# Two attention blocks on one core: output weights folded into the key-value sums, A's output kept in SBUF, full last units and a new instruction order

## The chip, the cores and the metric

One Trainium2 chip, one core. The kernel is one launch. Its time is device microseconds (us). Repeated executions of one kernel on one chip were compared with executions of the kernel before on the same chip in the same rounds. An execution is called slow when it lies over 1.5% above the fastest of its kernel, the others fast. The profile is one execution of its own, and its span is some 2 us shorter than the time of that execution (before: span 358.7, time 360.54).

## The reference

Two independent blocks, A and B, each on 2048 rows of 640 numbers in bf16, with 32 heads of 20 numbers. The two outputs are put side by side.

```python
def _A_ref(x, wqkv, wo):            # softmax attention
    qkv = (x @ wqkv).reshape(B, S, 3, H, Dh)      # then q, k, v by head
    scores = jnp.einsum("bhqd,bhkd->bhqk", q, k) * (Dh ** -0.5)
    p = _softmax(scores, axis=-1)
    o = jnp.einsum("bhqk,bhkd->bhqd", p, v)
    return o.transpose(...).reshape(B, S, D) @ wo

def _B_ref(x, wqkv, wo):            # linear attention
    phi = lambda t: jnp.where(t > 0, t + 1, jnp.exp(t)) + 1e-6
    pq, pk = phi(q), phi(k)
    kv = jnp.einsum("bhsd,bhse->bhde", pk, v)
    z = jnp.einsum("bhsd->bhd", pk)
    num = jnp.einsum("bhqd,bhde->bhqe", pq, kv)
    den = jnp.einsum("bhqd,bhd->bhq", pq, z)[..., None] + 1e-6
    return (num / den).transpose(...).reshape(B, S, D) @ wo
```

## The kernel before

The kernel does not compute A's 2048 x 2048 scores. It builds features of the keys (products up to third order), sums feature times value over all rows, builds the same features for the queries ("psi": sums and products of query rows loaded from a DRAM copy, f_Qd), and multiplies these with the sums. A "unit" is six heads by 512 query rows: twelve psi tiles against twelve tiles of sums (f_Tu). B runs beside it: key-value sums, query features, numerators and denominators.

A planner places every instruction when the program is built. It simulates the engines with assumed durations and transfer times, and when several tasks could be next it goes by a table of priorities (`_C`; a smaller number comes earlier). The result is one fixed order per engine and queue. So an edit of one step can move many other instructions.

The parts that matter here, first the end of B:

```python
        def qden(tc):                 # 512 query rows
            ...                       # 5 projections, features pqT, denominators
            m1 = self.spd([lambda e: e.dma_start(dc, self.dn[pr, :].rearrange(...))], ...)    # 32x512 -> 128x128
            e2 = self.dve(1.1, rc, (m1,), prio=0.9)                                           # reciprocal
            m2 = self.spd([lambda e, bdw=bdw: e.dma_start(bdw, dc)], (e2,), ...)              # to DRAM, f_Bd
        def numout(tc, qs, m2):
            for c in range(N_DC):     # 5 groups of 128 columns
                ...                   # 2 or 3 loads a group: reciprocals of each head to its rows, f_wB<-f_Bd
                def nmm(b, c=c):      # numerators: a block-diagonal product, 4 strips and 1 or 2 neighbours
                    self.fm(ps[:, b, :], self.kvN[:, c, 32:160], pqT[:, c, :], ...)
                    ...
                def npost(_, j=j, c=c, k=k):
                    sch.op("dve", lambda e: e.scalar_tensor_tensor(
                        oT[:, c, :], ps[:, j.bank, :], self.cn[:, c:c + 1], self.Rb[:, k, :], op0=ALU.add, op1=ALU.mult), ...)
            ...                       # out rows = oT x output weights woB
```

A's normalized output went to DRAM and back, to stand as 5 x 128 rows:

```python
        sch.op("dve", lambda e: e.tensor_tensor(self.OTw[0:120, ow], self.OTr[0:120, r:r + 3], self.Rbc[rb][0:120], op=ALU.mult), ...)
        fns = [lambda e: e.dma_start(bass.AP(od.tensor, od.offset, [[self.S, 120], [120 * self.S, nu], [1, 512]]),
                                     self.OTw[0:120, ow, 0:nu, :])]
        ...
    def t_out(self, qc, deps):
        ol = self.spd([lambda e: e.dma_start(self.OTp[:, k], self.Od.ap()[:, col].rearrange("(c p) q -> p c q", p=128))], ...)
```

And A's query weights were brought into their order by GpSimd:

```python
        def perm(_):
            for c in range(N_DC):
                sch.op("pool", lambda e, c=c: e.tensor_copy(
                    self.w[:, 0, c, 0:600].rearrange("p (b a h) -> p b a h", b=5, h=6),
                    self.w0r[:, c, 0:600].rearrange("p (b h a) -> p b a h", b=5, h=6)), ...)
```

## Time and profile before

| | before |
|---|---|
| time, median of 3 | 359.45 us (358.58 to 362.37) |
| span of the profile | 358.7 us |
| TensorE busy / idle | 303.6 / 55.1 us |
| VectorE, ScalarE, GpSimd busy | 253.3, 180.1, 31.3 us |
| DMA | 58.85 MB |
| TensorE holes over 1.9 us | 8, together 30.7 us |

### The profile page before, as it was taken

The numbers are of one execution on the slowest core, as the hardware profiler recorded it, in microseconds if no ns is written. First come the engines' busy times: TensorE is split into PE (matmuls) and PEld (weight loads), VectorE is DVE, ScalarE is ACT, GpSimd is POOL, SyncE is SP. The second block draws the span as 40 slices with busy tenths as digits, with TensorE's granted clock in tenths as the row PEclk, the third lists the DMA queues.
The fourth block names the chain that finished last, engine by engine and source line by source line (L and its number), as shares of the span: only waits on it lengthen the run. The fifth ranks groups of instructions, "written<-read, shape, count | busy, mean of one in ns | idle before, by whom it ended". The sixth has DMA issues, their size and how long they took to land.

```text
span 358.7 us, 14998 instructions
## 1 busy us (share of the span) xinstructions
PE 303.6 (85%) x6834; PEld 198.4 (55%) x6834; DVE 253.3 (71%) x350; ACT 180.1 (50%) x377; POOL 31.3 (9%) x49
## 2 busy tenths in 40 slices
PE   5989579999998899879988299982999868789955
PEld 2657347777764356546744178741554324658723
DVE  2589699999988986878896349795658767441330
ACT  2775647888884235444433235442355535335413
POOL 0049880000020100000000000000000000000000
PEclk9999989999999699998999879998799989999988
DMA  7999548214247258277736947579874466566642
GB/s 264 250 212 136 90 92 248 57 49 126 59 132 201 62 133 246 65 190 201 191 119 178 203 119 256 146 166 242 227 206 140 133 185 213 164 228 199 210 141 82
DMA packets 63571, 58.85 MB, mean 164 GB/s; under 512 B 21036, under 2 KB 59980, under 8 KB 63500
## 3 DMA queue, kind: packets, MB, share of 16 engines
q1 hardware_dynamic: 58940, 49.99, 53.9%
q10 hardware_dynamic: 4560, 7.83, 7.3%
q8 instruction: 55, 0.90, 1.2%
q14 instruction: 16, 0.13, 0.1%
HBM read 39.65 MB, written 14.48 MB: 151 GB/s over the span
## 4 chain that ended last, share of the span: by engine, by line
PE 53%; DMA 15%; DVE 11%; POOL 8%; SPq 6%; issue 5%; ACT 1%; ACTq 0%; DVEq 0%
PE ps L172 52%; DMA f_big<-f_Qd 4%; SPq L1594 4%; DMA f_w<-f_Od 4%; POOL f_w L1157 3%; POOL f_st L1248 3%; DMA f_Rc<-f_xT 2%; DMA f_dc<-f_dn 2%; DMA f_pk<-in_A_x_dram 2%; DVE f_Tu L1449 2%; DMA f_wB<-f_Bd 1%; DVE f_pk L1993 1%; DVE f_big L1607 1%; DVE f_big L1357 1%; DVE f_big L1362 1%
## 5 line engine op out<-in xcount | busy, mean ns | idle before, releaser
L1607 DVE TENSOR_TENSOR f_big<-f_big 120x1536 bf16<-120x1536 bf16 (+2 forms) x68 | 67.6, 1001 | 8.4 <-DMA f_big<-f_Qd 7.0
L172 PE MATMUL ps<-f_wB,f_xB 128*32 128x320 bf16 x1280 | 52.2, 311 | 10.1 <-issue 8.0
L172 PE MATMUL ps<-f_big,f_Tu 120*32 120x512 bf16 (+2 forms) x880 | 53.4, 384 | 3.1 <-issue 1.7
L172 PEld LDWEIGHTS ps<-f_wB,f_xB 128*32 128x32 bf16 x1280 | 37.5, 100 | 21.7 <-issue 9.6
L172 PE MATMUL ps<-f_w,f_xT 128*32 128x320 bf16 x1280 | 48.4, 307 | 0.4 <-issue 0.2
L172 PEld LDWEIGHTS ps<-f_w,f_xT 128*32 128x32 bf16 x1280 | 34.3, 100 | 11.3 <-issue 0.8
L172 PEld LDWEIGHTS ps<-f_big,f_Tu 120*32 120x32 bf16 (+2 forms) x880 | 27.7, 98 | 23.2 <-issue 3.1
L1092 ACT COPY f_xT<-ps 126x512 f32<-126x512 f32 (+1 forms) x30 | 17.4, 587 | 39.2 <-PE ps L172 32.8
L172 PE MATMUL ps<-f_wo,f_w 128*32 128x320 bf16 x640 | 25.6, 320 | 6.9 <-DMA f_w<-f_Od 6.9
L1762 ACT ACTIVATE f_ex<-ps 128x320 f32<-128x320 f32 (+1 forms) x52 | 25.7, 498 | 11.3 <-PE ps L172 6.4
L1357 DVE TENSOR_TENSOR f_big<-f_big,f_Ks 128x3200 bf16<-128x3200 bf16 x16 | 30.3, 1896 | 1.3 <-ACT f_Ks L1092 1.3
L172 PE MATMUL ps<-f_xT,f_w 128*32 128x512 bf16 (+2 forms) x440 | 28.8, 408 | 2.6 <-POOL f_w L1160 2.5
L1092 ACT CAST f_st<-ps 128x320 bf16<-128x320 f32 x32 | 13.3, 426 | 34.5 <-PE ps L172 30.2
L172 PE MATMUL ps<-f_woB,f_pk 128*32 128x320 bf16 x640 | 25.1, 312 | 6.4 <-DVE f_pk L1993 5.9
L1362 DVE TENSOR_TENSOR f_big<-f_big 128x3200 bf16<-128x3200 bf16 x16 | 29.7, 1857 | 0.0
L172 PE MATMUL ps<-f_xB,f_wB 128*32 128x512 bf16 x400 | 28.8, 392 | 0.6 <-ACT f_ex L1762 0.6
L1993 DVE SCALAR_TENSOR_TENSOR f_pk<-ps,f_cn,f_wB 128x512 bf16<-128x512 f32 x20 | 14.0, 745 | 21.7 <-PE ps L172 18.4
L1758 DVE TENSOR_SCALAR f_r<-ps 128x320 f32<-128x320 f32 x32 | 14.8, 485 | 18.2 <-ACT f_ex L1762 17.0
L1092 ACT CAST f_pk<-ps 128x320 bf16<-128x320 f32 x32 | 13.5, 429 | 26.1 <-PE ps L172 25.6
L172 PEld LDWEIGHTS ps<-f_wo,f_w 128*32 128x32 bf16 x640 | 19.3, 103 | 12.9 <-DMA f_w<-f_Od 7.9
L172 PEld LDWEIGHTS ps<-f_woB,f_pk 128*32 128x32 bf16 x640 | 17.8, 101 | 13.5 <-DVE f_pk L1993 7.9
L1627 ACT ACTIVATE f_Dq<-f_big 120x512 bf16<-120x512 bf16 (+1 forms) x24 | 15.1, 628 | 13.2 <-DMA f_big<-f_Qd 11.3
(125 smaller groups left out, 386.4 us busy)
## 6 DMA issues: line engine op xcount, KB each, us to landing
f_big<-f_Qd SPq DMA_DIRECT2D x20, 480.0 KB, 8.0
f_Qd<-f_OTw SPq DMA_DIRECT2D x40, 120.0 KB, 2.5
f_big<-f_Qd SPq DMA_DIRECT2D x20, 240.0 KB, 8.8
f_w<-f_Nd ACTq DMA_DIRECT2D x4, 720.0 KB
f_Rbc<-f_Nd ACTq DMA_DIRECT2D x4, 720.0 KB
f_wB<-f_Bd SPq DMA_DIRECT2D x12, 240.0 KB
f_w<-f_Od SPq DMA_DIRECT2D x4, 640.0 KB
out_dram<-f_st SPq DMA_DIRECT2D x16, 160.0 KB, 3.3
```

Source lines behind the costliest of these rows:

```text
L172: lambda e: e.matmul(out, lhsT, rhs, start=start, stop=stop, tile_position=tp, skip_group_check=sgc),
L1092: return self.sch.op("act", lambda e: e.copy(out, in_), reads=reads, writes=writes)
L1157: sch.op("pool", lambda e, c=c: e.tensor_copy(self.w[:, 0, c, 0:600].rearrange("p (b a h) -> p b a h", b=5, h=6), self.w0r[:, c, 0:600].re ...
L1248: ops.append((lambda e, x=x, a=a, n=n, b=b: e.tensor_copy(self.P[:, x, 6 * a:6 * (a + n)].rearrange("p (a h) -> p a h", h=6), self.ident[0 ...
L1357: sch.op("dve", lambda e: e.tensor_tensor(F[:, :, 122:222].rearrange("p h (d a) -> p h d a", a=20), k0.unsqueeze(2).broadcast_to([128, 32, ...
L1362: sch.op("dve", lambda e: e.tensor_tensor(F[:, :, 22:122].rearrange("p h (d a) -> p h d a", a=20), k0.unsqueeze(2).broadcast_to([128, 32, ...
L1594: fns.append(lambda e, x=x, d=d, st=st, nj=nj: e.dma_start(self.slot[0:40 * nj, s, x, :], self.q_load(5, qc, d, nj, st, False)))
L1607: return e.tensor_tensor(x[:, o:o + n, :], x[:, a:a + 1, :].broadcast_to([p, n, 512]), x[:, b:b + n, :], op=ALU.mult)
L1627: sch.op("act", lambda e: e.activation(self.Dq[0:120 if c < 5 else 40, dq, :], src, AF.Square), reads=(k0,), writes=(("Dq", dq),))
L1758: sch.op("dve", lambda e: e.tensor_scalar(r1, ps[:, j.bank, 0:n], 0.0, 1e-6, op0=ALU.max, op1=ALU.add), reads=(("ps", j.bank),), writes=(( ...
L1762: sch.op("act", lambda e: e.activation(ex, ps[:, j.bank, 0:n], AF.Exp), reads=(("ps", j.bank),), writes=(("ex", k, h),))
L1993: sch.op("dve", lambda e: e.scalar_tensor_tensor(oT[:, c, :], ps[:, j.bank, :], self.cn[:, c:c + 1], self.Rb[:, k, :], op0=ALU.add, op1=AL ...
```

## The change

Its intent is to take work and waits off TensorE's path. It has five structural parts, new assumed transfer times for the planner, and a new table of priorities. In the experiments below that exchange the table, the transfer times stay with the structure.

- B: M = (masked key-value sums) x (output weights) is built once. The output is then (query features x reciprocal denominators) x M, and the numerators go. The key sums z travel over DRAM to get the layout of the denominators' weights.
- Query features and M are ordered by place within a head, then by head, so the reciprocals of 32 heads are 32 rows, sent four times.
- A's normalized output is written straight into the operand of A's last projection; only heads 30 and 31 (40 of 640 rows) go over DRAM.
- These two heads, formerly four small units of 4 tiles, become full units over three or four row blocks.
- The query weights are permuted by ScalarE, for A and B.

```diff
-_C = dict(q=1.24, qs=0.0, ks=-0.005, kd=0.02, bk=1.83, bks=-0.005, bq=6.44, bo=0.03, out=0.46, pv=0.002,
-          fe=1.73, psi=5.5, r=-1.04, f=0.92, nm=2.51, op=2.71, kv=1.87, npo=2.33, bqs=0.002,
-          bd=-0.79, bn=3.42)
+_C = dict(q=1.06, qs=0.02, ks=0.02, kd=0.0, bk=1.32, bks=0.002, bq=0.33, bo=0.1, out=1.83, pv=0.05, fe=1.97,
+          psi=7.02, r=-4.28, f=0.38, nm=5.76, op=5.3, kv=1.49, npo=2.2, bqs=0.05, bd=0.02, bn=4.14)
 ... (A's query weights)
-                sch.op("pool", lambda e, c=c: e.tensor_copy(
+            self.copy(x.eng, self.w[:, 0, c, 0:600].rearrange("p (b a h) -> p b a h", b=5, h=6),
+                      self.w0r[:, c, 0:600].rearrange("p (b h a) -> p b a h", b=5, h=6), ("w0r",), (("w", 0, c),))
 ... (A's output)
+                sch.op("dve", lambda e: e.tensor_tensor(self.OTw[0:120, kw, c:c + nu, :], self.OTr[0:120, r:r + nu],
+                                                        self.Rbc[rb][0:120, 0:nu], op=ALU.mult), ...
-        self.ost[G] = self.spd(fns, (m,), (("OTw", ow),), (("Od", G),), prio=0.6)
 ... (B: the key sums, M, the denominators)
+        z1 = self.spd([lambda e: small(e, bass.AP(zd.tensor, zd.offset, [[1, 128], [128, N_DC], [1, 1]]), self.zn[:, 0, :])], ...
+        z2 = self.spd([lambda e: small(e, self.zn[:, 1, :], bass.AP(
+            zd.tensor, zd.offset, [[1, 4], [D_HEAD, N_HEADS], [4, N_DC], [1, 1]]))], (z1,), ...
+                        self.fm(ps[:, b, 0:320], self.KVT[:, c, 128 * k:128 * (k + 1)], self.woB[:, c2, hc], ...
-            m2 = self.spd([lambda e, bdw=bdw: e.dma_start(bdw, dc)], (e2,), (("dc", tc % 2),), (("Bd", tc),), ...
+            m2 = self.spd([lambda e, i=i: e.dma_start(self.Rb[32 * i:32 * i + 32, k, :].rearrange("h (j q) -> h j q", j=4), dc)
+                           for i in range(4)], ...
+                sch.op("dve", lambda e: e.scalar_tensor_tensor(
+                    pqT, pqT, 1e-6, self.Rb[:, k, :].unsqueeze(1).broadcast_to([128, N_DC, 512]), op0=ALU.add,
+                    op1=ALU.mult), ...
-                self.fm(ps[:, b, :], self.kvN[:, c, 32:160], pqT[:, c, :], start=True, stop=False, ...
+                            self.fm(ps[:, b, 0:320], pqT[:, c, 128 * tl:128 * (tl + 1)], self.Mp[:, c, hc], ...
```

## The prediction

> **What bounds the kernel now.** I began with the page: busy time by engine, and the span in 40 slices.
>
> ```profile
> PE 303.6 (85%) x6834; PEld 198.4 (55%) x6834; DVE 253.3 (71%) x350; ACT 180.1 (50%) x377; POOL 31.3 (9%) x49
> ...
> PE   5989579999998899879988299982999868789955
> ...
> PEclk9999989999999699998999879998799989999988
> ```
>
> TensorE is the busiest engine. Span minus its busy time is 358.7 - 303.6 = 55.1 us of idling. The slices put that in a few places: slices 4 and 5 (40 to 60 us), one at 200, one at 245, and the last quarter. So the time is matmul work plus holes. The table of stretches, cut at those places (columns: TensorE, weight load, VectorE, ScalarE, GpSimd busy us, granted clock, DMA share, GB/s), shows what a hole costs:
>
> ```profile
> 40.00:50.00 10.00, 5.92 (x132) 4.10 (x132) 10.00 (x7) 4.05 (x11) 9.82 (x4) 0.83 0.54 98
> ...
> 200.00:206.30 6.30, 0.04 (x4) 0.04 (x7) 0.87 (x3) 0.00 (x0) 0.00 (x0) 0.84 1.01 181
> 206.30:210.00 3.70, 3.70 (x53) 2.57 (x56) 0.00 (x0) 1.20 (x3) 0.00 (x0) 0.50 0.74 203
> 243.90:250.50 6.60, 0.08 (x8) 0.03 (x8) 3.82 (x5) 1.05 (x3) 0.00 (x0) 0.86 1.03 231
> 250.50:256.00 5.50, 5.50 (x88) 3.36 (x92) 3.13 (x3) 1.39 (x4) 0.00 (x0) 0.54 0.88 228
> ```
>
> After each of the two long holes the clock is about half for 4 to 5 us, and both holes have the DMA engines full (share 1.0). Summing idle TensorE time over 10 us stretches I get: 0-40: 6.7 us; 40-60: 6.6; 60-120: 2.6; 120-200: 7.0; 200-280: 14.6; 280-end: 17.7. The chain that ended last, in order of time (start, us, what), names what fills them:
>
> ```profile
> 39.85 2.50 POOL f_w L1157
> 42.40 2.75 POOL f_w L1157
> ...
> 236.94 13.48 DMA f_w<-f_Od
> ...
> 341.58 0.62 SPq L1972
> 342.24 4.98 DMA f_wB<-f_Bd
> ```
>
> GpSimd permutes A's query weights while Q projections wait; A's output goes to DRAM and back before its last projection; B's end waits for reciprocals broadcast from DRAM by 52 small loads, issued one after the other by SyncE. The VectorE timeline adds one thing: the same instruction before and inside the GpSimd permutation (39.9 to 52.1 us).
>
> ```profile
> 39.43 1.82 DVE L1357 TENSOR_TENSOR f_big<-f_big,f_Ks 128x3200 bf16<-128x3200 bf16 x1
> ...
> 43.95 2.88 DVE L1357 TENSOR_TENSOR f_big<-f_big,f_Ks 128x3200 bf16<-128x3200 bf16 x1
> ...
> 50.90 1.34 DVE L1269 SCALAR_TENSOR_TENSOR f_woB<-f_Rbc,f_pq 128x147 bf16<-128x147 int32 x1
> ```
>
> The product stretches from 1.82 to 2.88 us, the mask operation from 0.31 (at 39.20) to 1.34.
>
> **What the Trainium skill says.** "SBUF — State Buffer", Who interferes with whom: VectorE with two SBUF inputs and GpSimd lock each other out of a shared port pair. The stretched instructions above agree. "TensorE: Matmul & The Clock Gate", HAM oscillation: TensorE gaps above about 3.4 us bring the half clock back. The trace agrees (0.50 and 0.54 after gaps of 6.7 and 6.5 us). "DMA: Bandwidth & Descriptors", Anatomy of one DMA: a fixed cost of about 2 us on the GpSimd-issued path. These transfers are issued by SyncE and ScalarE and their small ones (64 KB, the denominators) land in 4.0 to 5.8 us, so I use those. The same page, Rules for kernel authors: a strided last dimension is one descriptor per element. That bears on the new 640-number transfers; nothing in this trace shows one.
>
> **The change, part by part.**
>
> *B's fold.* Per 512 rows the numerators took 5 groups of 4 matmuls and 8 single strips, 112 in all: 5.2 + 3.2 + 2.5 = 10.9 us (rows of f_kvN with f_xB, f_pq, f_Vp). They go, with 28 column sums (0.4). Instead the kernel builds M = (masked key-value sums) x (output weights) once: 30 transposing matmuls of 128 columns at 23 ns (the 147-column ones: 7.5 us / 320) = 0.7, and 26 groups x 4 = 104 matmuls of 320 columns at 39 ns (25.1 / 640) = 4.1 us. The output projection keeps its 640 matmuls, with normalized queries for numerators. On VectorE 20 x 745 ns = 14.0 us (L1993) go; 4 in-place products of 2560 elements come. Row L1781 takes 665 ns for 512 and 811 for 640, so 1.14 ns an element: 3.0 us each, 12.0 in all. SyncE loses 52 x 0.73 = 38 us of issuing and gets 16 issues.
>
> *Last heads as full units.* Four small units with 64 matmuls (4.2 us) go. Two units come: one full, (53.4 + 9.0) / 20 = 3.1 us, and one of 176 columns, 48 x 28 ns = 1.3. 8 more selector matmuls: about 1.0. On VectorE 4 x 1.3 = 5.2 becomes 3.2 + 1.1 = 4.3, and the normalizing products shrink from 14.0 to about 12.5. The six loads of each small unit (20 of 0.74 and 4 of 1.64 us, 21 us of issuing) become two per unit.
>
> *A's output in SBUF.* The round trip over f_Od (2.6 MB out, 2.6 back) goes, save 40 rows of 640.
>
> *Query rows by place then head.* 30 instead of 40 stored rows per head: 4.8 MB becomes 3.6.
>
> *Weights permuted on ScalarE.* 12.6 us leave GpSimd. ScalarE gets 5 x 0.8 us for A and 5 x 0.65 for B (597 ns for 608 columns, row f_Ks<-f_big), and with the copies of M about 15 us, on an engine with 180 of 359 busy. Q projections can start some 10 us earlier, and the VectorE stretching goes: 1.05 + 0.32 + 0.36 + 1.05 + 1.03 = 3.8 us.
>
> *Order.* All priorities and assumed transfer times are new; B's query projections now come early.
>
> Sums. TensorE: -10.9 - 0.4 - 4.2 + 0.7 + 4.1 + 3.1 + 1.3 + 1.0 = -5.3, so 298 us. VectorE: 253 - 14.0 + 12.0 - 3.8 - 0.9 - 1.5 = 245 us. DMA: out 5.1 (f_Bd) + 5.1 (f_Od) + 1.2 + 1.4 (small units) + 0.3; in 1.6 (M) + 1.0 (reciprocals) + about 0.3: net -10 MB of 58.85.
>
> TensorE stays the busiest, so the time is 298 plus its idling. By stretch, my judgement: 0-40: 6.7 to 5.5 (fewer GpSimd constants); 40-60: 6.6 to 1.5; 60-120: 2.6 unchanged; 120-200: 7.0 to 6; 200-280: 14.6 to 6 (the f_Od wait goes; the hole at 200 has no named releaser, but stood with full DMA engines, so I count half of it); 280-end: 17.7 to 11 (the SyncE-bound broadcast goes, the last store and one serial chain stay). That is 33 us. Fewer cold stretches take some 2 us off the busy time (3.7 x 0.50 + 5.5 x 0.46 = 4.4 today). 298 - 2 + 33 = 329. I add 5 us for waits that a new order will make and that I can't see: **334 us**.
>
> **Rivals.** *Only the matmul work counts.* New waits replace the old ones and only the 5.3 us are saved: about 353 us. For it: 85% busy, and queues that run in order wait wherever a transfer lands later than planned. Against: the three waits named on the chain are structurally gone. *A new chain at B's end.* The key-value sums (ready at 241 us) now feed two 640-number transfers over DRAM, the denominators, a transfer, a reciprocal, a broadcast and a 3 us product; beside that M goes out and back. Five serial landings of 5 to 8 us are some 35 us before B's first output. If the sums come late, the end is bare: about 362 us. Against: the assumed transfer times were raised (4 to 6, 6.5 to 8), and A's work can lie beside it. *ScalarE or VectorE holds the first stage.* VectorE is over 93% busy from 60 to 100 us; if ScalarE's added copies delay the key evictions, the gain of the first stage (5 us) is lost: about 340 us.
>
> **Range and chances.** The middle is 334. All holes closed down to about 20 us gives 318; the first rival 353. The range is 320 to 350. Faster by over 2% means below 352.3: 0.87. Same: 0.10. Slower: 0.03.
>
> **What would show it.** Right: TensorE busy 295 to 300 us; no f_kvN with 512 columns; no hole over 3 us at 40-60; no GpSimd permutation; VectorE 243 to 248; DMA about 49 MB; idling 28 to 40 us. Wrong: TensorE idle still near 50 us, with the new M, z or reciprocal transfers named in the last 80 us; or a TensorE busy time above 302.

## More of the kernel before

The experiments ran in three batches, each on a chip of its own with its own executions of the kernel before, so kernels of different batches are compared by their ratios to it and not by their times.

One more view is needed to compare with later. It lists what TensorE waited for. The columns are the total in us, the number of waits, and the longest; "issue" is a wait for which the profile names nothing.

```profile
PE ps L172 <- issue: 10.0, 6, 6.7
PE ps L172 <- DMA f_w<-f_Od: 6.9, 2, 6.5
PE ps L172 <- DVE f_pk L1993: 6.7, 7, 2.3
...
PE ps L172 <- DVE f_xB L1781: 4.8, 2, 3.4
...
PE ps L172 <- POOL f_w L1160: 2.5, 1, 2.5
```

These are, in order: a hole without a name at 200 us, A's round trip over DRAM, B's normalized numerators, B's late query features, and the weights permuted by GpSimd.

## The result

The changed kernel takes 326.08 us (median of 4, 325.31 to 329.35), the kernel before 359.01 us (4, 356.97 to 362.37) in the same rounds. The ratio is 0.912 (95% interval 0.903 to 0.921). A ratio here and below is the mean time of one kernel's fast runs over that of the kernel before's fast runs of the same rounds, so not quite the ratio of the medians quoted. All four runs of the changed kernel were fast; of the kernel before one, 362.37, counts as slow by the 1.5% rule.

The page of the changed kernel, busy time and slices:

```profile
PE 290.7 (90%) x6866; PEld 202.5 (63%) x6866; DVE 250.8 (78%) x342; ACT 191.7 (59%) x400; POOL 11.6 (4%) x35
...
PE   5989869998899989999999899999669949999994
...
PEclk9999968999999995999999999999979999999999
```

The span is 323.5 us, so TensorE idles 32.8 us; busy time fell by 12.9 us and idling by 22.3. A slice is 8.1 us; what is left of holes is in the sixth (40 to 49 us), in two at 226 to 243 and in one at 259 to 267. There are four holes over 1.9 us instead of eight, 12.5 us together. TensorE's waits, same columns as before:

```profile
PE ps L172 <- issue: 7.2, 9, 3.8
PE ps L172 <- ACT f_big L1091: 3.6, 2, 3.0
PE ps L172 <- DVE f_big L1592: 3.0, 1, 3.0
```

Of the four named waits of before none is left; what remains without a name has 7.2 us instead of 10.0. The table of stretches, cut at the new holes (TensorE, weight load, VectorE, ScalarE, GpSimd busy, granted clock, DMA share, GB/s):

```profile
41.28:44.30 3.02, 0.07 (x4) 0.00 (x0) 2.63 (x7) 2.96 (x6) 2.47 (x10) 0.87 0.41 91
44.30:49.00 4.70, 4.67 (x44) 1.71 (x48) 3.11 (x3) 3.10 (x7) 3.80 (x10) 0.50 0.59 87
223.00:233.98 10.98, 8.83 (x171) 5.93 (x172) 7.46 (x9) 5.79 (x16) 0.00 (x0) 1.00 0.73 39
233.98:237.75 3.77, 0.01 (x3) 0.00 (x1) 1.41 (x2) 0.00 (x0) 0.00 (x0) 1.00 0.78 156
```

The first hole is new in kind: ScalarE is busy in it and GpSimd no longer is the cause. Ahead of the second there is a stretch in which the DMA engines are 0.73 busy and move only 39 GB/s, where the holes of before had 181 and 231 GB/s. The chain that ended last, in order of time (start, us, what):

```profile
250.25 12.77 DMA f_dc<-f_dn
...
267.11 39.30 PE ps L172 x942
306.43 0.43 ACT f_Ks L1091
...
307.00 12.52 PE ps L172 x360
```

From 267 us on the chain is TensorE's own work. Before, the last 60 us of it were eviction, matmul, reciprocal transfer and again eviction by turns.

### The profile page after: what moved, and what is told of

The parts are those of the page before. It is cut to its first block, busy times and chain, and to the rows that moved or that the text cites. A ratio compares the mean times of both kernels' runs of the same rounds, so it can differ in the third digit from the quotient of the medians.

```text
span 323.5 us, 14990 instructions
## 1 busy us (share of the span) xinstructions
PE 290.7 (90%) x6866; PEld 202.5 (63%) x6866; DVE 250.8 (78%) x342; ACT 191.7 (59%) x400; POOL 11.6 (4%) x35
## 2 busy tenths in 40 slices
DMA packets 58757, 47.60 MB, mean 147 GB/s; under 512 B 23629, under 2 KB 57609, under 8 KB 58689
## 4 chain that ended last, share of the span: by engine, by line
PE 64%; DVE 11%; DMA 10%; ACT 9%; issue 3%; ACTq 1%; SPq 0%; DVEq 0%
PE ps L172 64%; DMA f_dc<-f_dn 4%; DVE f_big L1592 2%; ACT f_w L1091 2%; DVE f_big L1355 2%; DVE f_big L1360 2%; DVE f_Tu L1447 2%; DMA f_Nd<-f_Rc 2%; DMA f_pk<-in_A_x_dram 2%; DMA f_big<-f_Qd 2%; ACT f_Ks L1091 1%; ACT f_wB L1091 1%; ACT f_pk L1091 1%; ACT f_big L1091 1%; DVE f_kn L1365 1%
## 5 line engine op out<-in xcount | busy, mean ns | idle before, releaser
L1592 DVE TENSOR_TENSOR f_big<-f_big 120x1536 bf16<-120x1536 bf16 (+3 forms) x66 | 67.0, 1015 | 1.9 <-DMA f_big<-f_Qd 0.4
L172 PE MATMUL ps<-f_big,f_Tu 120*32 120x512 bf16 (+5 forms) x968 | 59.5, 377 | 6.3 <-issue 3.1
L172 PE MATMUL ps<-f_wB,f_xB 128*32 128x320 bf16 x1280 | 48.9, 299 | 2.1 <-ACT f_Vp L1091 1.4
L172 PEld LDWEIGHTS ps<-f_big,f_Tu 120*32 120x32 bf16 (+2 forms) x968 | 32.3, 97 | 26.1 <-issue 7.1
L1091 ACT COPY f_xT<-ps 126x512 f32<-126x512 f32 (+2 forms) x27 | 15.4, 576 | 43.9 <-PE ps L172 37.7
L1091 ACT CAST f_pk<-ps 128x320 bf16<-128x320 f32 (+4 forms) x65 | 26.0, 416 | 11.7 <-PE ps L172 11.4
L1767 ACT ACTIVATE f_ex<-ps 128x320 f32<-128x320 f32 (+1 forms) x52 | 25.6, 498 | 11.6 <-PE ps L172 5.4
L1605 ACT ACTIVATE f_Dq<-f_big 120x512 bf16<-120x512 bf16 (+1 forms) x22 | 13.6, 618 | 17.6 <-DMA f_big<-f_Qd 13.1
L172 PEld LDWEIGHTS ps<-f_wo,f_w 128*32 128x32 bf16 x640 | 18.5, 98 | 7.2 <-ACT f_xT L1091 2.1
L172 PEld LDWEIGHTS ps<-f_xT,f_w 128*32 128x32 bf16 (+2 forms) x440 | 12.2, 106 | 16.7 <-issue 5.7
L1091 ACT CAST f_qk<-ps 120x512 bf16<-120x512 f32 (+1 forms) x21 | 12.3, 585 | 14.8 <-PE ps L172 14.7
L172 PEld LDWEIGHTS ps<-f_xB,f_wB 128*32 128x32 bf16 x400 | 13.6, 96 | 11.7 <-issue 4.2
L1763 DVE TENSOR_SCALAR f_r<-ps 128x320 f32<-128x320 f32 x32 | 14.9, 486 | 7.2 <-ACT f_ex L1767 5.0
L1091 ACT COPY f_Ks<-f_big 128x608 bf16<-128x608 bf16 (+1 forms) x32 | 19.1, 597 | 1.0
```

The costliest lines, as they stand in the source:

```text
L172: lambda e: e.matmul(out, lhsT, rhs, start=start, stop=stop, tile_position=tp, skip_group_check=sgc),
L1091: return self.sch.op("act", lambda e: e.copy(out, in_), reads=reads, writes=writes)
L1592: sch.op("dve", lambda e: e.tensor_tensor(sl[:, o:o + n, :], sl[:, a:a + 1, :].broadcast_to([120, n, N]), sl[:, b:b + n, :], op=ALU.mult), ...
L1605: sch.op("act", lambda e: e.activation(self.Dq[0:120, dq, 0:N], sl[:, 0, :], AF.Square), reads=(k0,), writes=(("Dq", dq),))
L1763: sch.op("dve", lambda e: e.tensor_scalar(r1, ps[:, j.bank, 0:n], 0.0, 1e-6, op0=ALU.max, op1=ALU.add), reads=(("ps", j.bank),), writes=(( ...
L1767: sch.op("act", lambda e: e.activation(ex, ps[:, j.bank, 0:n], AF.Exp), reads=(("ps", j.bank),), writes=(("ex", k, h),))
```

## The experiments

In the original kernels the planner's order changes with everything else. So the first question is how much is the structure and how much the order. "Last B features" below is the start of the last VectorE product that makes a feature of B's queries.

**1. The old structure with the new table, and the new structure with the old table.**

```diff
 # before_newprio: the kernel before
-_C = dict(q=1.24, ... bq=6.44, ...)
+_C = dict(q=1.06, ... bq=0.33, ...)
 # after_oldprio: the changed kernel, the same lines the other way round
```

> The kernel before with only the new table of priorities; nothing structural changes. Theory S (the gain is structural: matmuls and round trips that are gone): the time stays within 2% of before, 352 to 366 us, TensorE busy stays near 303 us and idling stays near 50. Rival O (the new order made most of the gain): at or under 342 us, half of the 33 us.

> The changed kernel with only the old table of priorities. Theory S: at most 342 us, at least half of the gain is left, TensorE busy 289 to 296 us. Rival O: at or over 345 us, because TensorE idling goes back to about 50 us with the same 290 us of busy time.

before_newprio took 354.65 us (353.47 to 355.26, 4 runs, ratio 0.989, interval 0.982 to 0.995). after_oldprio took 355.23 us (351.68 to 358.75, 5 runs, two of them slow; ratio 0.981, 0.974 to 0.989). The kernel before took 359.38 (median of 11, three of them slow). By the 2% rule of the verdicts both halves are "unclear": at most a small gain. The two halves alone give 1.1% and 1.9%; together they give 8.8%. So the gain belongs to neither alone. In after_oldprio TensorE's busy time was 295.3 us, little above the changed kernel's, but it idled 20.5 us after 280 us, with one hole of 7.2 us that ended on a normalizing product of B (total, number and longest of these waits):

```profile
PE ps L172 <- DVE f_xB L2020: 8.8, 2, 7.2
```

That is the second rival of the prediction, the new chain bare at the end.

**2. One entry of the table.** In the changed kernel B's last query features start at 283.1 us; in after_oldprio at 326.1. (Columns: min, median, max ns of one; first and last start.)

```profile
L1786 DVE SCALAR_TENSOR_TENSOR f_xB<-f_ex,f_r x10: 683/688/693, 239.8 to 283.1; 128x512 bf16<-128x512 f32 x10
```

```profile
L1787 DVE SCALAR_TENSOR_TENSOR f_xB<-f_ex,f_r x10: 683/693/693, 292.1 to 326.1; 128x512 bf16<-128x512 f32 x10
```

So only `bq` was moved, once back and once forth.

```diff
 # after_lateq: the changed kernel
-bk=1.32, bks=0.002, bq=0.33,
+bk=1.32, bks=0.002, bq=6.44,
 # oldprio_earlyq: the changed kernel with the old table, but
-bks=-0.005, bq=6.44,
+bks=-0.005, bq=0.33,
```

> The changed kernel with one priority put back: B's query projections rank late again (bq 6.44 in place of 0.33). Theory Q (the new structure needs B's queries early, because denominators, reciprocals and normalization now stand in one row before any of B's outputs): 343 us or more, with TensorE holes of several us after 300 us that end with the normalizing products of f_xB. Rival (the whole table matters, no single entry): under 338 us.

> The changed kernel with the old table of priorities (355 us) but B's query projections early (bq 0.33). Theory Q: at most 340 us, half or more of the 29 us come back. Rival (the whole table matters): 346 to 356 us.

after_lateq took 344.09 us (340.98 to 344.88, 4 runs, ratio 0.964, 0.956 to 0.972), oldprio_earlyq 323.25 us (321.70 to 324.00, 4 runs, ratio 0.908, 0.901 to 0.914), the kernel before 357.04 (11 runs). By the ratios, one entry costs about 19 of the 32 us when it is put back (0.912 to 0.964). When it is the only new one it takes the ratio from 0.981 to 0.908, about 26 us, and that is as far as the whole table gets. Their last features, after_lateq and then oldprio_earlyq:

```profile
L1786 DVE SCALAR_TENSOR_TENSOR f_xB<-f_ex,f_r x10: 625/691/693, 268.6 to 315.4; 128x512 bf16<-128x512 f32 x10
```

```profile
L1787 DVE SCALAR_TENSOR_TENSOR f_xB<-f_ex,f_r x10: 623/682/693, 249.3 to 283.6; 128x512 bf16<-128x512 f32 x10
```

| kernel | last B features | last normalizing product | span | idle after 280 us |
|---|---|---|---|---|
| after_oldprio | 326.1 | 340.8 | 353.3 | 20.5 |
| after_lateq | 315.4 | 328.1 | 342.0 | 16.1 |
| changed kernel | 283.1 | 303.5 | 323.5 | 4.6 |
| oldprio_earlyq | 283.6 | 303.5 | 320.6 | 5.9 |

Where the features are late the span ends 27 us after the last of them. I take that for their own serial work (denominators, a transfer, a reciprocal, a broadcast, a product of 2.8 us, the outputs); its links were not timed one by one. Where they are early it ends 37 to 40 us after, and TensorE is busy meanwhile: the chain is covered.

**3. Does the old structure gain from the same entry?**

```diff
 # before_earlyq: the kernel before
-bks=-0.005, bq=6.44,
+bks=-0.005, bq=0.33,
```

> The kernel before with one entry of its priority table changed (B's query projections, 6.44 to 0.33), so B's query products should come at about 200 us instead of 231 to 266. My theory (the old structure can't use early queries, because its numerators wait for 52 reciprocal loads issued one after the other by SyncE, and the new structure needs them): within 2% of the kernel before, 352 to 364 us, with the numerators still ending at 320 us or later. Rival (the early queries are the gain, whatever the structure): 335 to 345 us, ratio 0.94 to 0.96.

It took 367.09 us (361.28 to 369.10, 4 runs, two of them slow by the 1.5% rule). Its two fast runs, 361.28 and 365.54, lie above the kernel before's median of 358.60 (7 runs), so it is not faster, and the rival (335 to 345) falls. But the edit hardly did what it was meant to do. The features of the first 512 rows were expected at about 200 us and came at 216.8 to 255.6 (before: 230.9 to 266.4), the last ones started at 296.9 (before: 307.8), and the key-value sums came late. The column sums of them, the first thing that TensorE does with them, start at 283.5 us; before at 242.4.

```profile
PE ps L172 <- DVE f_pk L1993: 15.1, 8, 6.8
```

After that the old end runs bare: TensorE waits 15.1 us for the normalized numerators, against 6.7 before. So this run does not settle the question. A run of experiment 1 does better, before_newprio, the old structure with the whole new table:

```profile
L1780 DVE SCALAR_TENSOR_TENSOR f_xB<-f_ex,f_r x10: 683/688/692, 250.7 to 285.4; 128x512 bf16<-128x512 f32 x10
```

Its last features start at 285.4 us, as early as the changed kernel's 283.1, and it still takes 354.65 us. With the old structure, early queries alone are worth little. That the 52 loads issued one after the other by SyncE also bind is an argument from the traces (in before_newprio, with the features of the first 512 rows at 205.7 to 223.7 us and the column sums at 227.6, the numerators still spread from 276.6 to 332.4), not a thing that a run took away.

**4. The matmul work that was removed.** The 112 matmuls of the old numerators were put back into the changed kernel, beside the denominators, into a bank that the denominators then overwrite. The order of all else stayed as it was.

```diff
 # after_extramm
             def dmm(b):
                 for c in range(N_DC):
+                    self.fm(ps[:, b, :], self.kvN[:, c, 32:160], pqT[:, c, :], start=True, stop=False, ...)
+                    ...      # and the neighbours, as in the old numerators
+                for c in range(N_DC):
                     sch.mm(ps[pr, b, :], self.kvZ[:, c, :], pqT[:, c, :], ...)
```

> The changed kernel with the 112 matmuls of the old numerators put back beside the denominators, their results overwritten; order otherwise the same. Theory (time is matmul work plus holes): TensorE busy rises by 9 to 11 us and the time by 8 to 11 us, to 334 to 337 us. Rival (these matmuls would fall into waits): the time rises by less than 5 us.

It took 327.15 us (323.38 to 332.80, 6 runs, one slow; ratio 0.915, 0.908 to 0.922). The changed kernel's ratio was 0.912, so the difference of 0.003 (about 1 us) is within what these rounds can tell. The rows of the added matmuls show 9.0 us of busy time (4.2 + 2.7 + 2.1), less than the 10.9 the prediction gave them. TensorE's busy time in this one execution rose by only 3.7 us, to 294.4, as the rest was shorter, and the span by 1.1, to 324.6. So the work fell into waits, as the rival said (under 5 us), and the expected 8 to 11 us lie outside the interval. The removal of the numerators' matmuls was worth about 1 us, give or take some 4.

**5. The permutation of the query weights.**

```diff
 # before_actperm: the kernel before, with the changed kernel's tasks on ScalarE
-                sch.op("pool", lambda e, c=c: e.tensor_copy(
+            self.copy(x.eng, self.w[:, 0, c, 0:600]..., self.w0r[:, c, 0:600]..., ("w0r",), (("w", 0),))
 # after_poolperm: the changed kernel, the same the other way round
 # before_actperm_fixed: the kernel before, planned as before, only emitted on the other engine
-                sch.op("pool", lambda e, c=c: e.tensor_copy(
+                sch.op("act", lambda e, c=c: e.copy(
```

> The kernel before with only A's query weights permuted on ScalarE in place of GpSimd. Theory of the prediction: the 6.6 us hole at 40-60 shrinks to under 3.5 us and VectorE loses 3.8 us of stretching, so 353 to 356 us (3 to 6 us less). Rival (time won there is only lost again at a later wait, since the order after it is planned, not earned): 357 to 361 us although the hole is gone.

> The changed kernel with A's query weights permuted on GpSimd again (B's stay on ScalarE). Theory: 329 to 333 us, 3 to 6 us more, VectorE products stretched again to over 2 us beside the GpSimd copies and a TensorE hole of 5 us or more at 40-60. Rival: 325 to 328 us, since ScalarE's copies were themselves on the chain (7.2 us from 36.8 to 44.0 us) and GpSimd's are no worse.

> The kernel before with A's query weights copied by ScalarE at the very place of the order where GpSimd copied them: order and everything else are the same, which the first try of this edit (369 us, all engines reordered by the planner) was not. Theory of the prediction: 353 to 357 us, VectorE products at 1.8 us again between 40 and 52 us. Rival L (the copies block the key evictions behind them on ScalarE): 359 to 364 us. If it is at or under 360 us, the 369 us of the first try came from the new order, not from the copies.

before_actperm took 369.33 us (361.82 to 370.97, 6 runs). The planner had moved so much that of TensorE's 6,834 matmuls in the trace only some 4,600 stand in the same order as before, and five of the six runs count as slow against the sixth, so it has no ratio; it tells nothing about the permutation, and that is its lesson. after_poolperm took 323.05 us (317.14 to 325.59, 6 runs; some 4,800 of 6,866 matmuls in the same order). Its ratio, 0.889 (0.881 to 0.897), rests on the two runs that count as fast; the other four lie between 322.6 and 325.6. It is at least not slower than the changed kernel. In its profile GpSimd permutes from 28.8 to 40.9 us and stretches a VectorE product to 2.9 us, and from 28 to 60 us TensorE idles 3.6 us, against 3.9 in the changed kernel. Neither engine closes the hole of this stage there; with GpSimd 2.7 us of it lie before 40 us. (The profile is of a run that counts as slow, 323.76 us.)

before_actperm_fixed is the clean one: every order is the planner's of before (VectorE's is the same in the trace, instruction by instruction). It took 358.31 us (354.77 to 360.94, 6 runs, one slow) against 357.04, ratio 1.007 (1.001 to 1.013). The product of 3200 elements was back at 1.82 us during the permutation, so the stretching did come from GpSimd. But ScalarE now spent 6.8 us on the copies while key tiles waited in PSUM for its evictions:

```profile
PE ps L172 <- ACT f_big L1092: 6.4, 2, 6.2
```

A TensorE wait of 6.2 us for ScalarE stands where holes of 4.4 us (ended by VectorE) and 2.5 us (ended by GpSimd) stood. In the changed kernel it is the same thing in smaller size, as its ScalarE timeline shows (start, us, operation, count):

```profile
36.67 7.29 ACT L1091 COPY f_w<-f_Tu 128x600 bf16<-128x600 bf16 x10
```

Ten copies in 7.29 us, 36.7 to 44.0, and TensorE's hole is 41.35 to 44.33.

**6. A's output over DRAM again.**

```diff
 # after_roundtrip: the changed kernel
         self.mult[G] = m
+        st = self.spd([lambda e: e.dma_start(dr, self.OTw[0:120, kw, c:c + nu, :])], (m,), (("OTw", kw, c),), (("Od", qc, c),), ...)
+        return self.spd([lambda e: e.dma_start(self.OTw[0:120, kw, c:c + nu, :], dr)], (st,), (("Od", qc, c),), (("OTw", kw, c),), ...)
```

> The changed kernel with A's packed output sent to DRAM and read back before A's last projection, as the kernel before did; the planner will move other instructions. Theory (the round trip of 13.5 us is hidden where the outputs of A have other work beside them; only DMA load and later A outputs come): 326 to 332 us, DMA about 5 MB more. Rival (keeping A's output in SBUF is a large part of the gain): over 335 us, with TensorE holes that end on the read of f_Od.

It took 337.05 us (334.71 to 343.67, 4 runs, one slow; ratio 0.938, 0.928 to 0.949), by the ratios about 9 us more than the changed kernel, with 52.56 MB instead of 47.60. My own theory said 326 to 332: it falls, the part is worth more than that. Some 6,150 of 6,866 matmuls stand in the same order. The waits:

```profile
PE ps L172 <- issue: 11.5, 4, 8.7
PE ps L172 <- DMA f_w<-f_Od: 4.1, 1, 4.1
```

Only 4.1 us are a wait for the round trip itself. The larger hole, 8.7 us at 225.4, has no name; the next experiment says what it is.

**7. The key sums as rows, not as single numbers.** In the changed kernel 640 four-byte numbers are written to DRAM one by one from 217.8 us and read back one by one. Here they are turned by TensorE first, written as 5 rows of 512 bytes and read as 128 rows of 80 bytes. This was done to the changed kernel and to oldprio_earlyq.

```diff
 # after_zrows, oldearlyq_zrows
-z1: 128 x 5 elements of 4 bytes;  z2: 128 x 5 elements of 4 bytes
+            sch.mm(ps[0:N_DC, b, 0:128], self.zb[:], self.ident[:], start=True, stop=True, ...)
+        z1 = self.spd([lambda e: e.dma_start(bass.AP(zd.tensor, zd.offset, [[128, N_DC], [1, 128]]), self.z5[:])], ...)
+        z2 = self.spd([lambda e, i=i: e.dma_start(self.zn[32 * i:32 * i + 32, :], bass.AP(
+            zd.tensor, zd.offset, [[D_HEAD, N_HEADS], [1, D_HEAD]])) for i in range(4)], (z1,), ...)
```

> The changed kernel, with the key sums sent over DRAM as 5 rows of 512 bytes and read back as 128 rows of 80 bytes, instead of 640 elements of four bytes each way. The planner may move other instructions. Theory (the 640 small writes keep the transfer queues slow from 218 to 232 us and delay the next instruction fetch, so that TensorE idles 3.8 us at 234): write and read together land in under 12 us instead of 18.5, no TensorE hole over 2 us at 225 to 245, 320 to 323 us, ratio to the changed kernel 0.98 to 0.99. Rival (the slow stretch comes from the many psi loads in flight, the small writes only suffer in it): the hole stays and the time is 325 to 328 us.

> The same edit of the key sums on the changed kernel with the old priority table and early B queries (323.3 us so far). Theory: 318 to 321 us. Rival (nothing gained): 322 to 325 us.

after_zrows took 322.20 us (320.44 to 324.21, 4 runs, ratio 0.897, 0.890 to 0.905); oldearlyq_zrows 325.93 us (324.53 to 326.84, 4 runs, ratio 0.909, 0.901 to 0.916), where it gained nothing (0.908 without). The two ratios of the changed kernel with and without were taken in different batches, 0.897 and 0.912, and their intervals overlap.

What the edit did is plainer in the transfers. The table is read from the DMA packets of each trace: the two fetches of instructions between which the hole begins (the instruction queue carries packets of 16,384 bytes), the longest packet of any kind between 210 and 240 us, and TensorE's hole without a name.

| kernel | fetches of instructions, us | longest packet | hole |
|---|---|---|---|
| before | 190.2, then 203.5 | 1.4 us (195 to 206 us) | 6.66 us at 199.6 |
| changed kernel | 222.3, then 235.4 | 4.7 us | 3.76 us at 234.0 |
| after_roundtrip | 217.8, then 231.6 | 4.8 us | 8.71 us at 225.4 |
| after_zrows | 224.3, then 231.6 | 1.5 us | none |

In the changed kernel 643 four-byte packets start between 220 and 225 us, and from 222.7 to 231.7 eighteen packets of 1,024 bytes (the psi loads) take 2.0 to 4.7 us each. after_zrows has 58 four-byte packets in those 5 us, no late fetch there, and its write and read of z landed in at most 11.6 us (230.1 to 241.7) instead of 18.5.

A count shows what the hole is. Take the matmuls and weight loads that TensorE has started, and subtract 256 for each 16,384-byte packet of the instruction queue that has landed. In none of the fourteen traces does that ever exceed 449. All eleven holes over 1.9 us without a name begin when it stands at 449 (once at 448), and end 1.3 to 1.5 us after the next of these packets lands. In the kernel before it is 449 at 199.6 us, after 8,385 starts and 31 packets; in the changed kernel at 234.0, after 10,177 and 38. So in these holes TensorE had run out of fetched instructions. The time between two fetches alone is no sign: in the changed kernel 13.1 us also pass between those of 115.7 and 128.8 us, without a hole.

What makes a fetch late is shown only in part. In the changed kernel the slow packets and the hole of 3.8 us went with the small writes. But the kernel before had its late fetch without such packets, with the DMA engines full (share 1.01 in the hole), oldearlyq_zrows, without the small writes, has a hole of 3.7 us of this kind at 156.8, and after_poolperm has the writes and a packet of 4.7 us but no such hole at that place: its count got no higher than 391 there.

The changed kernel's wait was not all gained: in after_zrows the sums wait for the turn on TensorE, z is complete 5.4 us later, and a hole of 6.3 us appears at 250.3. And since the slow stretch also lies in after_roundtrip, its 9 us are not the price of the round trip alone. A run with both edits would part them; that stays open.

## Why the prediction was right, and where it was not

The time fell inside the range, 8 us under the middle of 334. The sum of the prediction was 298 - 2 + 33 + 5.

- **TensorE's work, 5.3 us less: right, at 6.3.** In stretches at half clock a matmul takes twice its time (one of 320 columns 71 ns, outside them 35; kernel before), so half of the busy time that lies in half-clock stretches is the clock's: 29.1 / 2 = 14.5 us before, 15.9 / 2 = 7.9 after. At full clock that leaves 303.6 - 14.5 = 289.1 and 290.7 - 7.9 = 282.8. M's matmuls took 4.7 us (4.1 predicted), the transposing ones 0.7 (0.7), the normalizing products 2.82 us each (3.0). Put back, the numerators' matmuls took 9.0 us (10.9 priced).
- **The cold clock, 2 us less: the term that was mis-sized.** It fell by 14.5 - 7.9 = 6.6 us. The prediction counted only two stretches after long holes; five of the eight holes are followed by 3.4 us or more at half clock, and 10.1 of the 29.1 us (119 to 126 and 160 to 163 us) follow no such hole at all; in the 3.4 us before 119.0 TensorE was 0.59 busy, with no gap over 0.28 us.
- **Allowance for unseen waits, 5 us: not needed.** Without it and with the clock right the sum is 334 - 5 - 4.6 = 324.4, against the span of 323.5.
- **Idling of 33 us in total: right (32.8), by errors that cancel, so in part by luck:**

| stretch, us | before | predicted | changed kernel |
|---|---|---|---|
| 0 to 40 | 6.7 | 5.5 | 5.7 |
| 40 to 60 | 6.6 | 1.5 | 3.3 |
| 60 to 120 | 2.6 | 2.6 | 4.2 |
| 120 to 200 | 7.0 | 6 | 3.8 |
| 200 to 280 | 14.6 | 6 | 11.2 |
| 280 to end | 17.7 | 11 | 4.6 |

- **40 to 60 us, "Q projections can start some 10 us earlier, and the VectorE stretching goes": the step that failed.** The stretching went (1.82 us products in both runs with the permutation on ScalarE). The Q projections did start 8.2 us earlier (44.3 us for 52.5). The idling did not go, it shrank to 3.3 us and changed its cause, by the mechanism of the third rival: ScalarE's copies hold up the key evictions behind them. At fixed order the move gains nothing (experiment 5, +0.7%). The copies were put at 0.8 us from a row of 597 ns. That row's mean mixes 608 and 288 columns (the 608 alone take 0.73 us); the copies that permute took 1.3 us for 600 columns (A) and 1.4 us for 640 (B).
- **200 to 280 us, "I count half of it": the hole at 200 went and one of the same kind came at 234,** behind the new four-byte transfers. The prediction had named their shape and given them no cost in load on others (experiment 7).
- **280 to the end: right in kind, too careful in size, and the cause was underrated.** Against the rival of a bare chain at B's end the prediction named the raised transfer times and A's work beside it, and gave the order one sentence, without saying that early queries are what covers the chain. Experiments 1 and 2 show that they are most of the matter: the same structure takes 344 us when only that entry is put back and 355 (its fast runs 352 to 355) with the whole old table, near the rival's 362, and by the ratios the entry is worth 19 to 26 us.
- **"Only the matmul work counts": rejected, and more so than expected.** The work counts for less than its own size (experiment 4: 9.0 us of it for 1.1 us of span).
- **A's output in SBUF: right.** The wait of 6.9 us for f_Od is gone; putting the round trip back costs about 9 us, part of it through the slow stretch.
- **VectorE, 245 us: too low, 250.8.** The normalizing products that went were 14.0 us on the page (the "20 x 745 ns" beside it would be 14.9). The selector products of the fuller last heads (13.2 us against 11.6 before) were left out of its sum, and the planner gave VectorE about 3.8 us more of evictions. It did not bind. DMA came out at 47.60 MB (49 predicted).

The fastest versions seen are after_zrows (ratio 0.897), after_poolperm (0.889, on two fast runs) and oldprio_earlyq (0.908), against 0.912 of the changed kernel. They were measured in other rounds than it, and the one combination tried did not add up, so no order among them is claimed.

## What to carry to other kernels

A new structure and a new order can each be worth 1 to 2% and together 9%, because a structure that makes a longer serial chain pays only where its inputs come early enough for other work to cover the chain; look for the entry of the schedule that feeds the chain's head before judging the structure. Where a planner reorders everything, test a local edit with the order held fixed, and take a pair of plain variants for no evidence about the edit. Work taken from one engine and given to another ("it has room: 50% busy") must be placed against what that engine does in that very stretch.

## What the Trainium skill lacked or had wrong

- "Runtime: NRT & Kernel Launch", Instruction fetch mechanics, has instructions arriving in blocks of 256 over a DMA queue of their own, at a cost that is mostly hidden. The traces agree with the blocks: TensorE never starts more than 449 matmuls and weight loads beyond 256 for each landed packet. The cost was not always hidden: in the eleven holes where TensorE stood at this limit it lost 2.2 to 8.7 us each. The page names a stall for taken branches only; none that I found names a late fetch in straight code as the cause of a wait.
- "DMA: Bandwidth & Descriptors", Rules for kernel authors, has one descriptor per element for a strided last dimension. The trace agrees (643 four-byte packets within 5 us). It does not say what they do to others: packets of 1,024 bytes of another transfer then took up to 4.7 us (1.5 us at most where the small ones were gone), and the engines moved 39 GB/s while 0.73 busy.
- "TensorE: Matmul & The Clock Gate", HAM oscillation, gives gaps over about 3.4 us. Here the half clock came, for 3.4 us at least, at or just after the end of gaps of 2.25 us (before_newprio, 272.4 us) and 2.98 us (changed kernel, 41.4 us), and did not come after one of 3.01 us (264.1 us).
- "SBUF — State Buffer" says that each access which crosses to a new 16-byte line pays a penalty, and gives no figure for ScalarE. Here its copy of 128 x 600 bf16 numbers that reads with a stride took 1.3 us; one of 128 x 608 that reads runs of 19 numbers took 0.73.
